# Linear attention beside a gated feed-forward on one core: the weights' side work ordered anew, sums of keys and values stored in whole rows

## The chip, the cores and the metric

One core of one Trainium2 chip runs the whole kernel. The metric is device time in microseconds (us), the median of several executions. Before the change three runs gave 2463.45, 2466.1 and 2470.53 us, so the median is 2466.1 us. The profile is of one further execution.

## The reference, cut to what matters

The input x has 2048 rows of 1024 numbers in fp32. It is normalized, and two branches read it: linear attention with learned feature maps (32 heads of 32), and a SwiGLU feed-forward of width 3584.

```python
xn = (x - mean(x)) / sqrt(var(x) + 1e-5)
q, k, v = xn @ wqkv                              # 32 heads of 32
pq, pk = q @ w_phi, k @ w_phi                    # by head
phi_q = concat(softmax(pq), softmax(-pq))        # 64 features for each head
phi_k = concat(softmax(pk), softmax(-pk))
kv, z = phi_k.T @ v, sum_s(phi_k)                # by head
s = ((phi_q @ kv) / (phi_q @ z + 1e-6)) @ wo
b = (silu(xn @ w1) * (xn @ w3)) @ w2
out = x + s * silu(b)
```

## The kernel before, in words

**Seven products for eight.** A large product is cut into 2x2 blocks and done as seven block products, by the table ORDER: A11 with B11, A12 with B21, S2 with T2, S1 with T1, S3 with T3, S4 with B22 and A22 with T4. S1 to S4 are sums of blocks of x, T1 to T4 sums of blocks of weights. Each fp32 operand is split in two parts: ACT's copy casts to the upper part, DVE's subtraction makes the lower (`split`, L89 to 92). Three passes of the parts make one product, so one step is 12 matmuls of 128x512 (4 blocks of depth by 3 passes).

**First stage: gate and up, 392 steps** (`gate_up`, L573). Two halves of eight row tiles; in each, 28 column blocks f of w1 and w3 by seven products. The accumulators are PSUM banks a, b and c (one, two and two buffers), and what reads a bank (`read`) stands behind its step. Operands from the weights are made four steps ahead by `b_operands` (L262): two sums, then seven splits, with T1 and T4 made on the way.

**The opening** (L670 to 746) is an order written by hand for PE, ACT, DVE, POOL and SP: statistics and norms of eight row tiles, transposes (`first_turn`), splits (`first_split`), sums (`first_sums`) and steps 0 to 3, for which x comes from few tiles. In this stretch POOL makes the weights' sums. Beside it stand folds (`first_folds`, L315): a fold multiplies a block of the weights of keys or queries by the block diagonal of w_phi, so that keys come out of the projection as features' inputs. A fold is a load `wr` or into `room_b`, four matmuls `pw` of 128x128 fp32 (L249; the trace counts eight records), an ACT copy, and a store wk_d or wqo_d. There are 32 folds. Ten of the first 14 stand in the opening, two ahead of each of steps 5 and 6. From step 4 on, steps follow each other.

**Side work by step.** From step 14 the rest runs beside the steps, by a plan that says at which step an instruction is issued (`at`, with `room` which moves a piece to the next step with time left on DVE): four pairs of row tiles of the second half (`side_x`, starting at steps 14, 27, 40 and 53: statistics, transposes, seven splits and their stores xo_d1), the remaining folds (`side_fold`, a load at s0 and the matmuls ahead of step s0+4), eight units of the weights of keys and values (`side_kv`, L473: four loads by `load_kv`, L351, two sums, seven splits with their stores wkv_d), and stores of the first half's operands. Unit m loads at step 64 + 12m.

**What all of these share.** Their blocks come from one pool of 14 buffers (`xp`, tag "x", by `blk`): x's tiles xt and xf, S3, the folds' wr and the units' wkv and t2. Split parts come from another pool, of 11 (`quad`). All DMAs are issued by SP in the order of the program; a load whose buffer is still in use holds SP, and so every DMA behind it.

**Second stage: keys and values** (`heads`, L789): for each half c of the heads, eight pairs of row tiles. `kv` (L779) adds up phi_k.T @ v for 16 heads in one PSUM bank pkv, with two more columns in which a head's sum z lies. When a half is done `kv_out` (L836) copies the sums out: kva on ACT, zs on DVE, then four stores, one after each of the next products. A store is two DMAs of 32 partitions x 4 x 32 into kv_d and two of 32 partitions x 4 x 1 into z_d. For c = 0 they lie inside the second half's products. For c = 1 they lie in the rounds of the third stage.

**Third stage: the product by w2**, rounds r of seven half-size products (L1027, six matmuls each): `a_first` loads hr (512 KB, L881) for the next round and makes the first operands, `a_second` the rest, `load_b` (L874) loads the weights' operands. In rounds 0 to 5 SP's order is the order of the program. Round 1 ends with the last `kv` and `kv_out(1, pkv)`; each of the four rounds behind it issues one store.

**Last stage:** queries, attention by kvu (loaded at L1110) and the output projection. Its `po` products (L1137) read kvu; zb, loaded at L1098, is z spread over the partitions.

Of the kernel before, what the change touches and what calls it, by code (L numbers as in the profile page):

```python
# [17 lines left out]
P = 128  # L18
# [10 lines left out]
def tile_kernel(ctx: ExitStack, tc: tile.TileContext, x, wkT, wqT, wv, wphi, wo, w1, w3, w2, out):  # L29
# [50 lines left out]
    wqo_d = [[dram.tile([P, 2, 512], F, name=f"wqo_d{c}_{k}") for k in range(ND)] for c in range(2)]  # L80
    wo_d = [[dram.tile([P, 2, 512], F, name=f"wo_d{c}_{k}") for k in range(ND)] for c in range(2)]
    w2_d = [{n: dram.tile([P, 2, 2, 512], F, name=f"w2_d{kb}{n}") for n in BNAMES} for kb in range(NKB)]
    kv_d = dram.tile([2, 2, DH, 2 * G, DH], F, name="kv_d")
    z_d = dram.tile([1, 2, 4, 4, 2, DH], F, name="z_d")


# [2 lines left out]
    def split(hi, lo, src, by=None):  # L89

        nc.scalar.copy(hi, src)  # L91
        (by or nc.vector).tensor_sub(lo, src, hi.bitcast(F))  # L92
# [166 lines left out]
        nc.sync.dma_start(rw[:, 1], w3[f].rearrange("p (h k) n -> p h (k n)", h=2))  # L259
        return [rw[:, a, h] for a in range(2) for h in range(2)]  # L260

    def b_operands(rw, bo, eng=None):  # L262
        eng = eng or nc.vector
        b11, b21, b12, b22 = rw
        t2 = work.tile([P, 512], F, name="t2", tag="w")
        b_sums(b11, b12, b22, t2, eng)
        yield
        for _, _, n in ORDER:
            src = {"B11": b11, "B21": b21, "T2": t2, "T1": b11, "T3": b12, "B22": b22, "T4": b21}[n]
            bo[n] = quad("bo")  # L270
            split(bo[n][:, 0], bo[n][:, 1], src.rearrange("p (k n) -> p k n", n=P))
            if n == "B11":
                eng.tensor_sub(b11, b22, t2)
            elif n == "B21":
                eng.tensor_sub(b21, b21, t2)
            yield


# [92 lines left out]
    def at(step, f, d=after):  # L371
        d.setdefault(step, []).append(f)
# [116 lines left out]
    def side_fold(m, s0):  # L489
        wT, k, c, d = folds[m]  # L490
        w = []
        at(s0, lambda: w.append(load_w(wT, k, c)))
        at(s0 + 4, lambda: w.append(flat(fold(w[0], c))), before)
        if m < 16:
            at(s0 + 4, lambda: nc.scalar.copy(flat(w[0]), w[1]))
            at(s0 + 6, lambda: nc.sync.dma_start(d, flat(w[0])))
        else:
            store_quad(s0 + 4, wqo_d[c][k], lambda: w[1], "wqo")

    def side_split(d, src, s0):  # L500
        r = []
# [33 lines left out]
        at(s0, lambda: nc.sync.dma_start(xo_d[0][ANAMES[j]][:, q],  # L535
                                         ao[ANAMES[j]][:, :, :, q * P:(q + 1) * P].bitcast(F)))

    hs, FOLDS = [], 14
    FIRST_STEP = 14
    for i in range(4, 8):  # L540
        side_x(i, FIRST_STEP + 13 * (i - 4))
    for m in range(FOLDS, len(folds)):
        side_fold(m, FIRST_STEP + 40 + 6 * (m - FOLDS))
    for m in range(8):
        side_kv(m // 4, m % 4, FIRST_STEP + 50 + 12 * m)
    for m in range(28):
        side_store(m, FIRST_STEP + 45 + 4 * m)

# [118 lines left out]
        return read  # L667


    for f in range(2):  # L670
        bos[0, f] = {}
        gens[0, f] = b_operands(rws.pop(0), bos[0, f], nc.gpsimd)
    stats(mvs[0], 0, xs[0])
    stats(mvs[0], 1, xs[1])
    r0 = rstd(mvs[0])
# [4 lines left out]
        norm(mvs[0], sd, t, xs[t])  # L680
    stats(mvs[1], 1, xs[3])
    first_turn(0, 0)
    r1 = rstd(mvs[1])
    next(r1)
    first_turn(1, 0)
    first_split("A11", (0,))
    sd = next(r1)
    for t in range(2):
        norm(mvs[1], sd, t, xs[2 + t])
# [10 lines left out]
    for t in (2, 3):  # L700
        first_turn(t, 1)
    reads = [gate_up(0)]
    next(gens[0, 0])
    first_split("A12", (2, 3))
    reads.append(gate_up(1))
    for _ in range(3):
        next(gens[0, 1])
    reads[0]()
    first_folds(1)
    reads.append(gate_up(2))  # L710
    stats(mvs[2], 0, xs[4])
    stats(mvs[2], 1, xs[5])
    r0 = rstd(mvs[2])
    next(r0)
# [4 lines left out]
    for t in range(2):  # L719
        norm(mvs[2], sd, t, xs[4 + t])  # L720
    reads.append(gate_up(3))
    stats(mvs[3], 1, xs[7])
    r1 = rstd(mvs[3])
    next(r1)
# [4 lines left out]
    sd = next(r1)  # L729
    for t in range(2):  # L730
        norm(mvs[3], sd, t, xs[6 + t])
    first_folds(3)
    for t in (6, 7):
        first_turn(t, 0)
        first_turn(t, 1)
    first_sums("S1", (0, 1))
    first_sums("S2", (0, 1))
    first_split("S2", (0, 1))
# [2 lines left out]
    first_split("S2", (2, 3))  # L741
    for f in range(2):
        next(gens[0, f])
    for h in silus:
        nc.scalar.activation(h, h, AF.Silu)
    first_folds(FOLDS - 4 - at_fold)

    def first_late(n):
        ao[n] = slot(0, ANAMES.index(n))
        first_split(n)  # L750

    for k in (5, 6):
        at(k, lambda: first_folds(2), before)
    at(4, lambda: first_split("S1"))
    at(5, lambda: first_sums("S3"))
    at(6, lambda: first_late("S3"))
    at(7, lambda: first_sums("S4"))
# [76 lines left out]
        return pkv, False, last, e1, v1  # L834

    def kv_out(c, pkv):  # L836
        kva = work.tile([P, 8, DH], F, name="kva", tag="h1", bufs=2)
        zs = small.tile([P, 8], F, name="zs")
        nc.scalar.copy(kva, pkv[:, :, :DH])

        nc.vector.tensor_scalar_add(zs[:, :4], pkv[:, :4, DH], 1e-6)
        nc.vector.tensor_copy(zs[:, 4:], pkv[:, 4:, DH])

        def store(j):
            sl = slice(32 * j, 32 * j + 32)
            for s in range(2):
                nc.sync.dma_start(kv_d[j % 2, s, :, G * c + j // 2:G * c + G:2], kva[sl, 4 * s:4 * s + 4])
                nc.sync.dma_start(z_d[0, c, :, j, s].rearrange("g f -> f g"), zs[sl, 4 * s:4 * s + 4])

        return [lambda j=j: store(j) for j in range(4)]  # L850

# [192 lines left out]
    for r, new in enumerate(steps):  # L1046
        kb, i = new or (NKB, 0)
        end = kb == NKB - 1
        if r == 0:
            in_order(ENG.SP)  # L1050
        elif r == 6:
            in_order()
        if new is None:
            in_order(ENG.SP, ENG.Activation, ENG.DVE, ENG.Pool)
            xT = split_q(xf)
        if kb + 1 < NKB and 1 < i < 7:
            load_b(kb + 1, i - 2)
        parts = first
        if r + 1 < len(steps) - 1:
            first = a_first(*steps[r + 1])  # L1060
        bank = {}
        for b, an, bn in TURN:
            if an in FIRST:
                if new:
                    product(kb, i, bank, r, parts[2], b, an, bn)
            elif old:
                product(*old, banks, r, second, b, an, bn)
                if new is None:
                    load_wo(2 * BNAMES.index(bn))
                    load_wo(2 * BNAMES.index(bn) + 1)  # L1070
        if new:
            second = a_second(*parts) if r else ready[1]
        if out_now and r:
            out_now.pop()()
        if r == 1:

            kv(*pend)
            out_now += kv_out(1, pkv)
            late_rw += [rwp.tile([P, 2, 2, 512], R, name="late", tag="rw") for _ in range(2)]
        if i + 1 == len(pairs):  # L1080
            if end:
                for k in range(6):
                    load_wo(k)
            else:
                load_b(kb + 1, 5)
                load_b(kb + 1, 6)


        if end:
            if i:  # L1090
                gate(*pairs[i - 1])
            if i in (1, 2):
                for k in range(4 * i - 4, 4 * i):
                    load_wq(1, k, ring("wq1"))
            if i == 3:
                zb = [flat(ring("zb").bitcast(F)) for _ in range(2)]
                for c in range(2):
                    nc.sync.dma_start(zb[c], z_d[:, c].rearrange("o g j s f -> o (g j s f)").to_broadcast([P, D]))  # L1098
            if 1 < i < 6:
                for j, t in enumerate(pairs[i - 2]):  # L1100
                    load_wq(0, 2 * i - 4 + j, accp.tile([P, 2, 512], R, name="wq0", tag=f"acc{t}"))
            if i == 4:
                xf = load_q(0)
            elif i == 5:
                xT = split_q(xf)
            elif i > 5:
                if i == 6:

                    kvu = work.tile([P, 2 * G, DH], F, name="kvu", tag="h1", bufs=2)
                    nc.sync.dma_start(kvu, kv_d.rearrange("a s f g d -> (a s f) g d"))  # L1110
                es[7 - i] = queries(project_q(xT, 7 - i, "bka"), 7 - i)
            if i == 7:
                xf = load_q(1)
        old, banks = new, bank
# [9 lines left out]
    def attend(c, e):  # L1124


        po = ps.tile([P, 2, 512], F, name="po", tag="po", bufs=1)
        for q in range(2):
            pt = ps.tile([P, 4, P], F, name="pt2", tag="tr", bufs=3)
            for g in range(4):  # L1130
                nc.tensor.transpose(pt[:, g, :], e[:, (4 * q + g) * P:(4 * q + g + 1) * P], ident)  # L1131
            et = work.tile([P, 4, P], F, name="et", tag="w")
            nc.scalar.copy(et, pt)  # L1133
            for g in range(4):
                for hh in range(2):
                    sl = slice(64 * hh, 64 * hh + 64)
                    nc.tensor.matmul(po[32 * g:32 * g + 32, hh, q * P:(q + 1) * P], kvu[sl, G * c + 4 * q + g], et[sl, g],  # L1137
                                     start=True, stop=True, skip_group_check=True)
        oT = quad("oT")
        o4 = oT.rearrange("p u (h q) t -> p u h q t", q=2)  # L1140
        split(o4[:, 0], o4[:, 1], po[:, :, :2 * P].rearrange("p h (q t) -> p h q t", t=P))
        return oT
# [66 lines left out]
```

## Time and profile before

| | |
|---|---|
| median of three runs | 2466.1 us (2463.45 to 2470.53) |
| profiled execution | 2460.08 us, span 2458.3 us |
| granted TensorE clock, mean | 0.994 |
| busy: PE, DVE, ACT, POOL | 2401.5, 1777.1, 881.7, 197.5 us |
| DMA | 518.65 MB, mean 211 GB/s |

PE is the matmul engine, DVE VectorE, ACT ScalarE, POOL GpSimd; SP issues the DMAs. L with a number is a line of the kernel. A row of a timeline has the start, the time, the engine, the line and operation, the output and input, shape, the count, and in brackets the engine's idle time before it with what ended it. SPq is SP's sequencer: its time is that of issuing a DMA. A row of the windows gives, for a stretch, the busy time of PE, PE's weight loads, DVE, ACT and POOL with the count of instructions, then the granted clock, the DMA engines' share and GB/s.

### The profile page before, as it was taken

How to read it: one execution, taken by the hardware profiler on the slowest of the kernel's cores; microseconds unless marked ns; L12 is line 12 of the kernel's file. 1: busy time of each engine (PE TensorE's matmuls, PEld its weight loads, DVE VectorE, ACT ScalarE, POOL GpSimd, SP SyncE). 2: the span in 40 equal slices, each digit the busy share in tenths (PEclk: the TensorE clock that was granted, in tenths of full speed). 3: DMA queues.
4: the chain of work that ended last, by engine and by line, in shares of the span. 5: the costliest groups of instructions: out<-in, count | busy, mean ns of one | idle time of the engine just before them, and what ended most of it. 6: DMA issues, size and time to landing. Idle time of an engine off the chain costs nothing. (4 is left out here: it accounts for less than half of the span.)

```text
span 2458.3 us, 35680 instructions
## 1 busy us (share of the span) xinstructions
PE 2401.5 (98%) x13648; PEld 1969.6 (80%) x13648; DVE 1777.1 (72%) x2893; ACT 881.7 (36%) x1549; POOL 197.5 (8%) x161
## 2 busy tenths in 40 slices
PE   6999989999999999999999998999999999999999
PEld 5888868888888888888787886888888887787777
DVE  7777767876588887764555665578788787777775
ACT  5545434444345454433111123422222243222221
POOL 2000000000000000000000000011111112232222
PEclk9999999999999999999999999999999999999999
DMA  7456879986888886665968756733454376223222
GB/s 269 144 197 233 275 270 319 317 301 220 265 296 305 299 294 230 243 231 213 349 186 330 247 174 154 208 97 135 171 180 172 119 276 233 89 73 96 73 86 69
DMA packets 299514, 518.65 MB, mean 211 GB/s; under 512 B 24400, under 2 KB 171856, under 8 KB 297552
## 3 DMA queue, kind: packets, MB, share of 16 engines
q1 hardware_dynamic: 299344, 516.38, 61.8%
q8 instruction: 107, 1.75, 0.3%
q14 instruction: 63, 0.52, 0.1%
HBM read 330.43 MB, written 185.87 MB: 210 GB/s over the span
## 5 line engine op out<-in xcount | busy, mean ns | idle before, releaser
L92 DVE TENSOR_TENSOR bo<-rw,bo 128x512 fp32r<-128x512 f32 x336 | 232.9, 695 | 163.1 <-ACT bo L91 162.3
L91 ACT CAST bo<-rw 128x512 fp32r<-128x512 f32 x336 | 206.4, 618 | 4.6 <-PE bankb L600 2.2
L1027 PE MATMUL bankb<-bo,as 128*128 128x512 f32 x816 | 201.7, 390 | 1.1 <-DVE acc L1039 1.1
L100 PE MATMUL pm<-wq,xh 128*128 128x512 f32 x768 | 185.5, 394 | 0.0
L1027 PEld LDWEIGHTS bankb<-bo,as 128*128 128x128 f32 x816 | 153.7, 188 | 33.6 <-DVE acc L1039 1.6
L100 PEld LDWEIGHTS pm<-wq,xh 128*128 128x128 f32 x768 | 141.9, 188 | 31.4 <-issue 3.0
L600 PE MATMUL bankb<-op0S,bo 128*128 128x512 f32 x672 | 163.7, 393 | 1.2 <-ACT op0S L91 0.8
L600 PE MATMUL bankb<-op0A,bo 128*128 128x512 f32 x672 | 161.6, 395 | 3.1 <-ACT op0A L91 1.9
L600 PE MATMUL bankc<-op0S,bo 128*128 128x512 f32 x672 | 162.9, 392 | 0.0
L600 PE MATMUL bankb<-op1S,bo 128*128 128x512 f32 x672 | 161.3, 389 | 0.0
L600 PE MATMUL bankc<-op1S,bo 128*128 128x512 f32 x672 | 161.3, 389 | 0.0
L600 PE MATMUL bankb<-op1A,bo 128*128 128x512 f32 x672 | 157.9, 390 | 0.4 <-DVE bo L92 0.2
L1027 PE MATMUL bankc<-bo,as 128*128 128x512 f32 x576 | 147.6, 392 | 8.3 <-ACT acc L1033 8.3
L600 PEld LDWEIGHTS bankb<-op0A,bo 128*128 128x128 f32 x672 | 126.2, 190 | 29.5 <-ACT op0A L91 2.1
L600 PEld LDWEIGHTS bankb<-op0S,bo 128*128 128x128 f32 x672 | 125.7, 189 | 28.1 <-ACT op0S L91 1.2
L600 PEld LDWEIGHTS bankb<-op1A,bo 128*128 128x128 f32 x672 | 125.8, 188 | 27.9 <-DVE u L642 1.2
L600 PEld LDWEIGHTS bankb<-op1S,bo 128*128 128x128 f32 x672 | 126.1, 188 | 26.2
L600 PEld LDWEIGHTS bankc<-op1S,bo 128*128 128x128 f32 x672 | 126.1, 188 | 26.2
L600 PEld LDWEIGHTS bankc<-op0S,bo 128*128 128x128 f32 x672 | 126.1, 189 | 26.2 <-DVE op0S L92 0.3
L100 PE MATMUL pm<-wos,oT 128*128 128x512 f32 x576 | 136.2, 389 | 0.0
L1027 PEld LDWEIGHTS bankc<-bo,as 128*128 128x128 f32 x576 | 108.8, 189 | 31.4 <-ACT acc L1033 8.8
L100 PEld LDWEIGHTS pm<-wos,oT 128*128 128x128 f32 x576 | 108.0, 188 | 22.7 <-issue 0.2
(222 smaller groups left out, 4256.7 us busy)
## 6 DMA issues: line engine op xcount, KB each, us to landing
rw<-in_w SPq DMA_DIRECT2D x112, 512.0 KB, 5.6
hr<-h_d SPq DMA_DIRECT2D x56, 512.0 KB, 3.6
h_d<-h SPq DMA_DIRECT2D x111, 256.0 KB, 5.1
xoS<-xo_d0S SPq DMA_DIRECT2D x32, 512.0 KB, 9.9
xoS<-xo_d1S SPq DMA_DIRECT2D x32, 512.0 KB, 6.6
room<-in_w SPq DMA_DIRECT2D x56, 256.0 KB, 6.9
xoA<-xo_d0A SPq DMA_DIRECT2D x24, 512.0 KB, 8.0
xoA<-xo_d1A SPq DMA_DIRECT2D x24, 512.0 KB, 4.1
```

Of the source, the lines that this page charges most:

```text
L91: nc.scalar.copy(hi, src)
L92: (by or nc.vector).tensor_sub(lo, src, hi.bitcast(F))
L100: nc.tensor.matmul(p, xT[dch][:, a], w(dch, b), start=n == 0, stop=n == 3 * ND - 1)
L600: nc.tensor.matmul(bank[b], bos[tb, f][bn][:, w, k], ao[an][:, u, k], start=first and n == 0, stop=LAST[b] == an and n == 11, skip_group_c ...
L1027: nc.tensor.matmul(bank[b], t[:, u, pos + k], bos[kb, bn, k][:, w], start=first and n == 0, stop=LAST[b] == an and n == 5, skip_group_chec ...
```

## The change

**Sums of keys and values.** kv_d is laid out anew, so that a store of one half is one DMA from kva with 512 bytes for each piece. z is transposed on PE (`pz`, in pkv's bank tag), copied by ACT into zt, and stored by two DMAs of 16 rows of 128 bytes. kv_out returns one store, three DMAs in all, in place of four stores with 16. kvu is loaded by four DMAs, and the index at L1137 follows.

**Side work.** Twelve folds, not 14, stand in the opening. The other 20 load from step 62 on, 5.5 steps apart (before: 18 from step 54, 6 apart), and are used five steps after their load. Unit m of the weights of keys and values loads at step 73 + 11m.

**Opening.** Folds are spread: one behind step 0's matmuls, one ahead of step 2's, two behind step 2's, two behind step 3's, two ahead of and two behind the last transposes, none behind step 4. The two silus of steps 0 and 1 move from ahead of step 4 to step 5. The subtractions that make T1 and T4 (`hold`) wait on POOL until both blocks' sums are done, and POOL's sums of the second block wait, by a copy of one column into `consts`, for the statistics of the fifth row tile. The first row tile's split A11 comes ahead of the second one's transpose.

```diff
-    kv_d = dram.tile([2, 2, DH, 2 * G, DH], F, name="kv_d")
+    kv_d = dram.tile([4, DH, 2, 2, 4, DH], F, name="kv_d")
...
-    def b_operands(rw, bo, eng=None):
+    def b_operands(rw, bo, eng=None, hold=None):
...
+            late = []
             if n == "B11":
-                eng.tensor_sub(b11, b22, t2)
+                late.append(lambda: eng.tensor_sub(b11, b22, t2))
             elif n == "B21":
-                eng.tensor_sub(b21, b21, t2)
+                late.append(lambda: eng.tensor_sub(b21, b21, t2))
+            if hold is not None:
+                hold += late
+            else:
+                for do in late:
+                    do()
             yield
...
-        at(s0 + 4, lambda: w.append(flat(fold(w[0], c))), before)
+        at(s0 + 5, lambda: w.append(flat(fold(w[0], c))), before)
         if m < 16:
-            at(s0 + 4, lambda: nc.scalar.copy(flat(w[0]), w[1]))
-            at(s0 + 6, lambda: nc.sync.dma_start(d, flat(w[0])))
+            at(s0 + 5, lambda: nc.scalar.copy(flat(w[0]), w[1]))
+            at(s0 + 7, lambda: nc.sync.dma_start(d, flat(w[0])))
         else:
-            store_quad(s0 + 4, wqo_d[c][k], lambda: w[1], "wqo")
+            store_quad(s0 + 5, wqo_d[c][k], lambda: w[1], "wqo")
...
-    hs, FOLDS = [], 14
+    hs, FOLDS = [], 12
...
     for m in range(FOLDS, len(folds)):
-        side_fold(m, FIRST_STEP + 40 + 6 * (m - FOLDS))
+        side_fold(m, FIRST_STEP + 48 + 11 * (m - FOLDS) // 2)
     for m in range(8):
-        side_kv(m // 4, m % 4, FIRST_STEP + 50 + 12 * m)
+        side_kv(m // 4, m % 4, FIRST_STEP + 59 + 11 * m)
...
+    held = []
     for f in range(2):
         bos[0, f] = {}
-        gens[0, f] = b_operands(rws.pop(0), bos[0, f], nc.gpsimd)
+        gens[0, f] = b_operands(rws.pop(0), bos[0, f], nc.gpsimd, held)
...
     first_turn(0, 0)
+    first_split("A11", (0,))
+    first_turn(1, 0)
     r1 = rstd(mvs[1])
     next(r1)
-    first_turn(1, 0)
-    first_split("A11", (0,))
...
     reads = [gate_up(0)]
+    first_folds(1)
     next(gens[0, 0])
     first_split("A12", (2, 3))
     reads.append(gate_up(1))
+
+    stats(mvs[2], 0, xs[4])
+    nc.gpsimd.tensor_copy(consts[:, 1:2], mvs[2][:, 0, 0:1])
     for _ in range(3):
         next(gens[0, 1])
+    for do in held:
+        do()
     reads[0]()
     first_folds(1)
     reads.append(gate_up(2))
-    stats(mvs[2], 0, xs[4])
+    first_folds(2)
     stats(mvs[2], 1, xs[5])
...
     reads.append(gate_up(3))
+    first_folds(2)
...
-    first_folds(3)
+    first_folds(2)
     for t in (6, 7):
         first_turn(t, 0)
         first_turn(t, 1)
+    first_folds(2)
...
-    for h in silus:
-        nc.scalar.activation(h, h, AF.Silu)
-    first_folds(FOLDS - 4 - at_fold)
...
-    for k in (5, 6):
-        at(k, lambda: first_folds(2), before)
+    def first_silus():
+        for h in silus:
+            nc.scalar.activation(h, h, AF.Silu)
+
     at(4, lambda: first_split("S1"))
+    at(5, first_silus)
     at(5, lambda: first_sums("S3"))
...
-        kva = work.tile([P, 8, DH], F, name="kva", tag="h1", bufs=2)
+        kvz = work.tile([P, 512], F, name="kvz", tag="h1", bufs=2)
+        kva, zt = kvz[:, :8 * DH], kvz[:8, 8 * DH:8 * DH + P]
         zs = small.tile([P, 8], F, name="zs")
-        nc.scalar.copy(kva, pkv[:, :, :DH])
+        nc.scalar.copy(kva.rearrange("p (m d) -> p m d", d=DH), pkv[:, :, :DH])
...
-        def store(j):
-            sl = slice(32 * j, 32 * j + 32)
+        pz = ps.tile([P, 512], F, name="pz", tag="kv", bufs=1)
+        nc.tensor.transpose(pz[:8, :P], zs, ident)
+        nc.scalar.copy(zt, pz[:8, :P])
+
+        def store():
+            nc.sync.dma_start(kv_d[:, :, :, c].rearrange("j f s m d -> (j f) s (m d)"),
+                              kva.rearrange("p (s n) -> p s n", s=2))
             for s in range(2):
-                nc.sync.dma_start(kv_d[j % 2, s, :, G * c + j // 2:G * c + G:2], kva[sl, 4 * s:4 * s + 4])
-                nc.sync.dma_start(z_d[0, c, :, j, s].rearrange("g f -> f g"), zs[sl, 4 * s:4 * s + 4])
-
-        return [lambda j=j: store(j) for j in range(4)]
+                nc.sync.dma_start(z_d[0, c, :, :, s], zt[4 * s:4 * s + 4].rearrange("g (j f) -> g j f", f=DH))
+
+        return [store]
...
-                    kvu = work.tile([P, 2 * G, DH], F, name="kvu", tag="h1", bufs=2)
-                    nc.sync.dma_start(kvu, kv_d.rearrange("a s f g d -> (a s f) g d"))
+                    kvu = work.tile([P, 2, G, DH], F, name="kvu", tag="h1", bufs=2)
+                    for a in range(2):
+                        for h in range(2):
+                            sl = slice(64 * a + 32 * h, 64 * a + 32 * h + 32)
+                            nc.sync.dma_start(kvu[sl].rearrange("f j g d -> f j (g d)"),
+                                              kv_d[a::2, :, h].rearrange("j f c m d -> f j (c m d)"))
...
-                    nc.tensor.matmul(po[32 * g:32 * g + 32, hh, q * P:(q + 1) * P], kvu[sl, G * c + 4 * q + g], et[sl, g],
+                    nc.tensor.matmul(po[32 * g:32 * g + 32, hh, q * P:(q + 1) * P], kvu[sl, g % 2, 4 * c + 2 * q + g // 2], et[sl, g],
```

On ACT in the opening, from the last transposes of row tiles 2 and 3 to the second square root (sd). xf is a transposed block, bo an operand from weights, op0A one from x, h a copy of a bank; room_b<-pw and wr<-pw are folds. Before:

```order
L222 COPY xf<-pt 128x512 x2
L91 CAST bo<-rw 128x512
L91 CAST op0A_275<-xf 128x4x128 x2
L91 CAST bo<-rw 128x512 x2
L626 COPY h_508<-bankb 128x512
L322 COPY room_b<-pw 128x512
L199 ACTIVATE sd<-mv,consts 128x2
L626 COPY h_551<-bankb 128x512
L199 ACTIVATE sd<-mv,consts 128x2
```

And of the kernel after the change, the same stretch:

```order
L222 COPY xf<-pt 128x512 x2
L328 COPY room_b<-pw 128x512
L91 CAST bo<-rw 128x512
L91 CAST op0A_275<-xf 128x4x128 x2
L91 CAST bo<-rw 128x512 x2
L632 COPY h_521<-bankb 128x512
L328 COPY room_b<-pw 128x512
L328 COPY wr<-pw 128x512 x2
L199 ACTIVATE sd<-mv,consts 128x2
L632 COPY h_576<-bankb 128x512
L328 COPY room_b<-pw 128x512 x2
L199 ACTIVATE sd<-mv,consts 128x2
```

One fold's copy now stands ahead of the casts of step 1's operands, two more ahead of the first square root and two ahead of the second.

On SP in the side work, where a unit of weights loads its four wkv. Of before this is unit 2, at step 88; wr_2905 is the block of the fold ahead of step 94:

```order
L258 DMA rw_2806<-in_w1 128x1024
L259 DMA rw_2806<-in_w3 128x1024
L535 DMA xo_d0A12_89<-op0A12_275 128x8x128
L354 DMA wkv_2857<-wk_d0_2_118 128x512
L355 DMA wkv_2859<-in_wv 128x512
L354 DMA wkv_2858<-wk_d0_6_122 128x512
L355 DMA wkv_2860<-in_wv 128x512
L436 DMA wkv_d0B11_102<-wkvo_2797 256x1x512
L436 DMA wkv_d0B21_103<-wkvo_2826 256x1x512
L242 DMA wr_2905<-in_wqT 128x512
```

After the change unit 1, at step 84, whose loads follow that of a fold's block, wr_2714, which the fold ahead of step 89 reads:

```order
L242 DMA wr_2714<-in_wqT 128x512
L360 DMA wkv_2716<-wk_d0_1_117 128x512
L361 DMA wkv_2718<-in_wv 128x512
L360 DMA wkv_2717<-wk_d0_5_121 128x512
L361 DMA wkv_2719<-in_wv 128x512
L442 DMA xo_d1A11_95<-xoA11_2648 128x1024
L226 DMA xn_d_57<-xf_2679 128x4x128
L502 DMA wk_d1_7_131<-wr_2544 128x512
L442 DMA xo_d1A12_96<-xoA12_2681 128x1024
L226 DMA xn_d_57<-xf_2712 128x4x128
L564 DMA h_d0_2_60<-h0_2514 128x4x128
L564 DMA h_d0_2_60<-h1_2491 128x4x128
```

The unit's loads stood ahead of stores of the unit before and of a fold's load; now they stand ahead of stores of x (xo_d1, xn_d), of a fold (wk_d) and of h.

On SP in the first rounds of the third stage. Before, from round 2's loads, with the first store, to round 3's loads (the four rows kv_d and z_d stand in each of the four rounds 2 to 5):

```order
L874 DMA bo<-w_d1B_187 128x1024 x2
L881 DMA hr<-h_d_0_58 128x1024
L847 DMA kv_d<-kva 32x4x32
L848 DMA z_d<-zs 32x4x1
L847 DMA kv_d<-kva 32x4x32
L848 DMA z_d<-zs 32x4x1
L874 DMA bo<-w_d1B_188 128x1024 x2
L881 DMA hr<-h_d_0_65 128x1024
```

After the change:

```order
L894 DMA bo<-w_d1B_187 128x1024 x2
L901 DMA hr<-h_d_0_58 128x1024
L865 DMA kv_d<-kvz 256x1x128
L868 DMA z_d<-kvz 16x1x32 x2
L894 DMA bo<-w_d1B_188 128x1024 x2
L901 DMA hr<-h_d_0_65 128x1024
L894 DMA bo<-w_d1T_189 128x1024 x2
```

Sixteen DMAs of kv_d and z_d in four rounds have become three in one.

More of the change, by code (lines that the diff above doesn't have):

```diff
@@ L743, in tile_kernel @@
         next(gens[0, f])
-    for h in silus:
-        nc.scalar.activation(h, h, AF.Silu)
-    first_folds(FOLDS - 4 - at_fold)
+    assert at_fold == FOLDS
     def first_late(n):
```

## The prediction, made before the result was known

> **What bounds the kernel now.** I read the windows first. PE is the bound almost everywhere, so only stretches in which it falls behind can give time back (busy PE in the second column, the granted clock third from the end):
>
> ```profile
> span 2458.3 us, 35680 instructions
> 0.00:80.00 80.00, 56.03 (x298) 47.19 (x298) 59.97 (x116) 44.25 (x83) 14.82 (x19) 0.94 0.72 248
> 80.00:300.00 220.00, 220.00 (x1022) 182.63 (x1021) 170.90 (x293) 106.59 (x189) 0.00 (x0) 1.00 0.63 211
> 300.00:400.00 100.00, 89.53 (x408) 74.35 (x407) 71.21 (x112) 44.95 (x83) 0.00 (x0) 0.95 0.87 294
> 400.00:1300.00 900.00, 896.33 (x4700) 739.28 (x4699) 649.44 (x991) 366.70 (x662) 1.83 (x14) 1.00 0.78 268
> 1500.00:1600.00 100.00, 90.51 (x450) 73.89 (x449) 53.80 (x102) 36.66 (x70) 2.59 (x2) 0.95 0.67 165
> ```
>
> Three stretches lose PE time, and the change touches all three: the opening, 24 us of 80; the middle of the first stage, 10.5 of 100; the start of the third stage, 9.5 of 100. Around them PE is full. In each loss the granted clock falls too, so a loss costs its idle time and some slow matmuls behind it.
>
> **The middle.** PE's timeline, then SP's, then one row of ACT and one of the list of transfers (its last column the time from issue to landing):
>
> ```profile
> 304.27 1.05 PE L249 MATMUL pw<-bd,wr 128*128 128x128 f32 x8
> 305.08 2.98 PE L600 MATMUL bankb<-op0S,bo 128*128 128x512 f32 x12
> ...
> 316.06 2.88 PE L600 MATMUL banka<-op0A,bo 128*128 128x512 f32 x12
> 318.78 2.88 PE L600 MATMUL bankb<-op0S,bo 128*128 128x512 f32 x12
> 332.10 2.04 PE L249 MATMUL pw<-bd,wr 128*128 128x128 f32 x8 [10.44 <-DMA wr<-in_wqT]
> 333.80 3.71 PE L600 MATMUL bankc<-op0S,bo 128*128 128x512 f32 x12
> ```
> ```profile
> 302.90 0.42 SPq L535 DMA_DIRECT2D xo_d0A<-op0A  x1
> 316.13 0.33 SPq L354 DMA_DIRECT2D wkv<-wk_d  x1
> ...
> 323.15 0.33 SPq L355 DMA_DIRECT2D wkv<-in_wv  x1
> 323.54 1.26 SPq L436 DMA_DIRECT2D wkv_d0B<-wkvo  x2
> 328.90 0.34 SPq L242 DMA_DIRECT2D wr<-in_wqT  x1
> ```
> ```profile
> 327.53 0.62 ACT L91 CAST wkvo<-wkv 128x512 fp32r<-128x512 f32 x1 [5.16 <-DMA wkv_d0B<-wkvo]
> ```
> ```profile
> wr<-in_wqT SPq DMA_DIRECT2D x3, 256.0 KB, 8.5
> ```
>
> SP issues nothing from 303 to 316 and four loads of unit 2 by 323.15: they wait for blocks of the pool of 14, which the last pair of x still holds. Behind them stand the unit's stores, on which ACT waits (issued from 323.54, landed by 327.53, so 4.0 us from first issue), then the fold's block wr. PE waits for wr 10.44 us. The slow clock adds 2.04 - 1.05 on the fold and 3.71 - 2.88 on the step: 1.8. The stall costs 12.3 us.
>
> **The start of the third stage.** SP's timeline, the transfers, the window, PE's timeline, and rows of the timeline of all engines:
>
> ```profile
> 1512.48 0.38 SPq L881 DMA_DIRECT2D hr<-h_d  x1
> ```
> ```profile
> hr<-h_d SPq DMA_DIRECT2D x4, 512.0 KB, 17.8
> ...
> kv_d<-kva SPq DMA_DIRECT2D x8, 16.0 KB, 9.7
> z_d<-zs SPq DMA_DIRECT2D x8, 0.5 KB, 11.5
> ```
> ```profile
> 1520.00:1530.00 10.00, 4.45 (x20) 3.36 (x18) 0.00 (x0) 0.00 (x0) 0.00 (x0) 0.83 1.02 207
> ```
> ```profile
> 1518.84 1.52 PE L1027 MATMUL bankc<-bo,as 128*128 128x512 f32 x6
> 1532.79 2.93 PE L1027 MATMUL bankc<-bo,as 128*128 128x512 f32 x6 [8.35 <-ACT acc L1033]
> 1535.52 3.53 PE L1027 MATMUL bankb<-bo,as 128*128 128x512 f32 x12
> 1548.36 1.66 PE L1027 MATMUL bankb<-bo,as 128*128 128x512 f32 x6 [1.15 <-DVE acc L1039]
> ```
> ```profile
> 1530.33 0.62 ACT L91 CAST af<-hr 128x512 fp32r<-128x512 f32 x1 [12.05 <-DMA hr<-h_d]
> ```
>
> The named releaser, ACT's copy, had itself waited 12.05 us behind a cast for hr. A store of half a kilobyte takes 11.5 us to land, and hr 17.8 (1512.48 to 1530.3), in a window in which the DMA engines are full at 207 GB/s. PE loses 8.35 + 1.15 idle and, at the slow clock, 2.93 - 1.52 and 3.53 - 2.88 (the twelve matmuls of a step above): 11.6 us.
>
> **The change part by part: stores of the sums.** Thirteen of 16 DMAs go, and kva's pieces of 128 bytes and zs's of 4 become 256 of 512 and 32 of 128. What is added on PE is one transpose of 128x8 for each half. No row shows this shape; between nothing and a quarter of a fold's 1.05 us, I take 0.3 each, the upper end. They wait for zs:
>
> ```profile
> 1509.17 1.20 PE L1027 MATMUL bankb<-bo,af 128*128 128x512 f32 x4
> 1509.77 0.15 DVE L842 COPY zs<-pkv 128x4 f32<-128x4 f32 x1
> ```
>
> The transpose stands behind four matmuls, which end about 1510.3, after zs at 1509.9; zt's copy comes behind an already queued cast on ACT. If that cover were gone, PE would wait about 1 us. For c = 0 PE showed no wait, and nothing is gained. kvu's four loads replace one, with a whole round of products ahead of their first reader; nothing. So the gain is 11.6 - 0.6 = 11.0. Its ends: 0, if the pieces were not the cause, and 12.5, if nothing is added and a last micro-wait goes.
>
> The row says that 16 KB in 128-byte pieces land in 9.7 us and 0.5 KB in 11.5, so cost goes by pieces, not by bytes. The Trainium skill, "DMA: Bandwidth & Descriptors", section "Why small descriptors are slow (HBM only)", gives each packet a small fixed overhead of about three cycles; by that alone, as an estimate, small pieces would be a minor load here, and the sum would be 2460 in place of 2449. That is the second rival.
>
> **The opening.** PE's, ACT's and DVE's timelines:
>
> ```profile
> 24.53 4.15 PE L600 MATMUL bankb<-op0A,bo 128*128 128x512 f32 x10 [1.23 <-DVE op0A L92]
> 28.52 2.91 PE L600 MATMUL banka<-op0A,bo 128*128 128x512 f32 x12
> 55.60 2.07 PE L249 MATMUL pw<-bd,room_b 128*128 128x128 f32 x8 [5.48 <-ACT room_b L322]
> 57.32 3.68 PE L600 MATMUL bankb<-op0S,bo 128*128 128x512 f32 x12
> 73.55 0.73 PE L600 MATMUL bankb<-op0S,bo 128*128 128x512 f32 x2 [0.79 <-ACT op0S L91]
> ```
> ```profile
> 71.32 2.18 ACT L91 CAST op0S<-room_a 128x512 fp32r<-128x512 f32 x4 [2.35 <-DMA wk_d<-room_b]
> ```
> ```profile
> 27.29 3.47 DVE L92 TENSOR_TENSOR bo<-rw,bo 128x512 fp32r<-128x512 f32 x2
> 41.27 1.92 DVE L212 TENSOR_SCALAR late_x<-late_x,mv,sd 128x512 f32<-128x512 f32 x4
> 52.22 1.28 DVE L92 TENSOR_TENSOR bo<-t,bo 128x512 fp32r<-128x512 f32 x2
> ```
>
> I followed the new order by hand with these durations. While POOL makes the weights' sums a DVE subtraction takes 1.74 (27.29's two), later 0.64 (52.22's two); I take POOL for the cause. With POOL held, step 0's matmuls go on at 23.3, 1.2 earlier. Then the third fold's copy on ACT stands ahead of the casts of step 1's operands: step 1 at about 31.0, 2.5 later than 28.52. Folds follow between steps 2 and 3, and their copies ahead of both square roots; the last norms end at 48.6 in place of 43.2 (41.27 + 1.92). From norms to the operands of step 4 it took 10.3 (43.2 to 53.5, the end of the row at 52.22). With about 1 us of waits step 4 starts at 59.9, 2.6 later than 57.32: today it starts late, behind silus and folds on ACT, and that 3.8 of slack takes up the rest. From there steps 4 to 7 stand without the four folds (3.2 us) and without the 2.35 us wait of the split of S3, which stands behind stores from room_b: step 8 at about 72.3, 1.8 earlier than the 73.55 (plus 0.5 of waits, about 74.1). Two of the 14 folds now run beside later steps, where each costs PE 0.81 (304.27 to 305.08): 1.6 back, and 0.2 is left, taken as nothing. Ends: 7 gained, if the copies find ACT free and step 1 isn't late; 5 lost, if two more steps run at half clock.
>
> **Side work.** All units load later, and unit 2's loads come after the last of x's splits; so the stall at 320 as it was goes. But the order shows another of the same kind. At step 84 the fourth load of unit 1 takes the block of wr_2714, which is loaded just ahead of it and read by the fold ahead of step 89. SP stands there until that fold is done. Queued behind are the stores of xo_d1, xn_d and wk_d1_7. At step 88 DVE makes S3 and S1 of the last pair of x in blocks which those stores must leave first. Behind them on DVE is the read of bank b, for which PE's step 90 waits.
>
> From rows: call the fold's end zero. The stores follow from 0.4 us on (0.42 an issue, as at 302.90); wk_d, the fourth, is issued at 1.2 and lands 4.0 later (the wkvo stores above), at 5.2. Three DVE instructions of about 0.65 bring the read to 7.2. PE has step 89 to do, 2.72 us (318.78 less 316.06). So PE is idle 4.5 us and loses about 1.5 at the slow clock, by the 1.8 above: 6.0. What stands further back, the block for the fold ahead of step 94, has four steps of cover left, 10.9 us, against 8.5 to land; nothing, but 5.3 if it is issued only behind DVE's late read, at 7.7 (7.7 + 8.5 - 10.9). The gain is 12.3 - 6.0 = 6.3; the ends are 1 (12.3 - 6.0 - 5.3) and 12.3 (DVE does not come late).
>
> **The sum.** 2460.1 - 0 - 6.3 - 11.0 = 2442.8 for an execution like the profiled one, which took 2460.08 (span 2458.3 and 1.8 around it). The median of the three runs is 6.0 above it, at 2466.1. So 2442.8 + 6.0 = 2448.8, forecast 2449.
>
> **The rivals.**
> 1. The middle's stall stays as large: SP's hold at step 84 delays the fold's block of step 94 as well, PE waits twice, and 5.3 of the 6.3 go: 2454. For it: SP's backlog stands ahead of that block, stores of h among it, which wait for DVE.
> 2. Small pieces are not the cause: hr was late since bo, hr and the late loads together filled the engines (207 GB/s at full share). Then the 11.0 go: 2460. Against it: hr brings 512 KB, which at 207 GB/s is 2.5 us, and three such loads issued together, 1.5 MB, would be done in 7.6, not in 17.8. The rule of the Trainium skill named above, of a small fixed overhead, would make this rival of it.
> 3. The opening loses about 6: ACT's fold copies ahead of casts and square roots are later than reckoned, and the steps after run at half clock as the 4.15 at 24.53 does: 2455.
> 4. The opening gains about 7: 2442.
> 5. Slower: the hold of SP repeats at every later unit. Each unit's last load could again take a block that a fold still has to read; if the six units from the third on lose as the one at step 84 does, 6 x 6 = 36 is added: 2485. It turns the sign from 17.3 / 6 = 2.9 us a unit on. Against it: later waits name blocks of steps well past, and from 400 to 1300 PE lost only 3.7 of 900 us.
>
> **How the numbers follow.** A measurement of this kernel can tell about 0.3% from no change, 7.4 us. The forecast has 0.52, with a range of its own of 2442 to 2455 (middle 1 to 12.3 and opening within 3). Rival 1 has 0.12, rival 2 0.08, rival 3 0.10, rival 4 0.12 and rival 5 0.06. Faster by over 0.3% (below 2458.7) are all but 2 and 5; of those a small part of 1 and 3 falls within 0.3%, and part of rival 2 to faster: 0.85 faster, 0.09 the same, 0.06 slower. The range reaches from 2438, where the middle costs nothing (6 less) and 5 of rival 4's 7 come too, to 2459, with rivals 1 and 3 and the edge of rival 2 inside; rival 5, most of 2 and the tails are left out, under 2 in 10.
>
> **What the profile after would show.** Right: the start of the third stage has hr landing in under 8 us and no wait of PE over 2; SP's row for the fourth wkv load of unit 1 stands behind a fold at step 89, and PE waits 3 to 6 us at step 90 with ACT or DVE as the releaser; the opening's step 4 starts at 58 to 62 and step 8 at 70 to 75. Wrong: hr still late beside three DMAs (rival 2), a wait for wr as long as before (1), or waits that repeat every 11 steps from 100 on (5).

## The result

The kernel after takes 2447.38 us, the median of six runs (2445.02 to 2449.6); before takes 2466.23 in six (2463.45 to 2470.53). The ratio is 0.9923, with an interval of 0.991 to 0.9936: faster, by 16 to 22 us. The forecast was 2449. One of the ten executions of before_new_opening below took 5340.17 us, far outside the other nine (2465.17 to 2469.96), and is left out of its ratio.

### The profile after

The profiled execution took 2447.39 us. First the windows, with the columns as before:

```profile
span 2445.6 us, 35679 instructions
0.00:80.00 80.00, 54.20 (x278) 44.91 (x279) 55.87 (x115) 42.44 (x80) 14.53 (x20) 0.89 0.70 235
80.00:300.00 220.00, 220.00 (x1017) 182.40 (x1017) 170.06 (x291) 106.99 (x190) 0.00 (x0) 1.00 0.59 199
300.00:400.00 100.00, 93.76 (x430) 77.55 (x428) 75.11 (x118) 46.82 (x86) 0.00 (x0) 0.98 0.92 315
1500.00:1600.00 100.00, 100.00 (x503) 82.49 (x503) 62.72 (x115) 41.66 (x80) 5.18 (x4) 1.00 0.47 170
```

The start of the third stage is full now (90.51 before), the middle has a smaller hole (93.76 in place of 89.53), and the opening has 1.8 us less of busy PE (54.20 in place of 56.03, at a clock of 0.89), of which 1.6 are the two folds that moved out of it.

**The third stage.** PE's timeline, then the list of transfers between 1508 and 1550:

```profile
1508.77 1.19 PE L1047 MATMUL bankb<-bo,af 128*128 128x512 f32 x4
1509.80 0.27 PE L861 MATMUL pz<-ident,zs 128*8 128x128 f32 x1
1509.82 0.70 PE L1047 MATMUL bankb<-bo,af 128*128 128x512 f32 x2
```
```profile
hr<-h_d SPq DMA_DIRECT2D x5, 512.0 KB, 5.3
kv_d<-kvz SPq DMA_DIRECT2D x1, 128.0 KB, 2.1
```

hr lands in 5.3 us, where it took 17.8, the transpose costs 0.27, and PE waits for nothing. To compare runs I take one number from PE's timeline: the time from the start of the last pkv group to the start of the 301st product matmul of this stage behind it (without the transpose). It is 80.82 us before and 68.97 after: 11.85 less.

**The middle.** SP's timeline, then DVE's, then PE's:

```profile
293.44 0.32 SPq L360 DMA_DIRECT2D wkv<-wk_d  x1
307.97 0.33 SPq L361 DMA_DIRECT2D wkv<-in_wv  x1
308.39 0.38 SPq L442 DMA_DIRECT2D xo_d1A<-xoA  x1
308.87 0.39 SPq L226 DMA_DIRECT2D xn_d<-xf  x1
309.35 1.14 SPq L502 DMA_DIRECT2D wk_d<-wr  x1
```
```profile
313.83 0.69 DVE L232 TENSOR_TENSOR s<-xf 128x512 f32<-128x512 f32 x1 [6.64 <-DMA wk_d<-wr]
314.55 0.69 DVE L234 TENSOR_TENSOR xf<-xf 128x512 f32<-128x512 f32 x1
315.16 0.68 DVE L648 TENSOR_TENSOR u<-bankb,u 128x512 f32<-128x512 f32 x1
```
```profile
306.89 1.05 PE L249 MATMUL pw<-bd,wr 128*128 128x128 f32 x8
307.69 2.98 PE L606 MATMUL bankc<-op0S,bo 128*128 128x512 f32 x12
315.90 7.19 PE L606 MATMUL bankb<-op0A,bo 128*128 128x512 f32 x24 [5.23 <-DVE u L648]
```

The rows read as a chain. SP issues nothing between 293.8 and 307.97, where the fold ends; wk_d goes out fourth, at 309.35; DVE's sum S3 waits for it until 313.83 and the read of bank b until 315.16; PE waits 5.23. Two steps, 24 matmuls, take 5.60 at full clock, here 7.19, so the stall costs 6.8, where the old one cost 12.3.

**The opening.** PE's timeline, one row of ACT's, one of DVE's, then the row of PE with which step 12 begins in the profile of before:

```profile
23.09 2.56 PE L606 MATMUL bankb<-op0A,bo 128*128 128x512 f32 x10 [0.25 <-DVE op0A L92]
...
52.60 1.86 PE L249 MATMUL pw<-bd,wr 128*128 128x128 f32 x8 [2.29 <-DMA wr<-in_wkT]
60.56 8.70 PE L606 MATMUL bankb<-op0S,bo 128*128 128x512 f32 x24 [6.10 <-ACT bo L91]
69.10 5.60 PE L606 MATMUL bankc<-op0S,bo 128*128 128x512 f32 x24
74.54 0.61 PE L606 MATMUL bankb<-op0S,bo 128*128 128x512 f32 x2
...
86.10 8.32 PE L606 MATMUL bankb<-op0A,bo 128*128 128x512 f32 x36
```
```profile
54.50 0.59 ACT L328 COPY wr<-pw 128x512 f32<-128x512 f32 x1 [3.57 <-PE pw L249]
```
```profile
45.56 1.92 DVE L212 TENSOR_SCALAR late_x<-late_x,mv,sd 128x512 f32<-128x512 f32 x4
```
```profile
85.30 8.32 PE L600 MATMUL bankb<-op0A,bo 128*128 128x512 f32 x36
```

Step 4 starts at 60.56 and steps 4 and 5 run at the slow clock, 8.70 in place of 5.60. Step 8 starts at 74.54 and step 12 at 86.10, 0.8 later than before (85.30). One profile says little here: in the eight profiles with this opening (after, after_old_stores, before_new_opening, small_kv, small_z, both z_extra kernels and unit_a_step_later, all below) step 12 starts between 82.97 and 87.70, on average at 85.3, and in the three with the old one at 85.30, 85.37 and 85.60. So up to step 12 the new opening gains and loses nothing on average.

**Where the two profiles differ.** Their spans differ by 12.7 us: 12.3 behind the last pkv group and 0.4 ahead of it. Ahead of it the middle gives 5.5 and the opening takes 0.8 and two folds 1.6; the other 2.7 are lost behind the middle and at the start of the second stage, mostly in small waits. The medians differ by 18.9. The rest lies with the execution of before that was profiled (2460.08, below its six timed runs), as the experiments show.

### The profile page after: what moved, and what is told of

Same layout as the page of the kernel before. It is cut to its first block, busy times and chain, and to the rows that moved or that the text cites. A ratio compares the mean times of both kernels' runs of the same rounds, so it can differ in the third digit from the quotient of the medians.

```text
span 2445.6 us, 35679 instructions
## 1 busy us (share of the span) xinstructions
PE 2401.9 (98%) x13650; PEld 1969.5 (81%) x13650; DVE 1774.3 (73%) x2893; ACT 882.6 (36%) x1551; POOL 197.1 (8%) x162
```

## The experiments

Each is timed in rounds with the kernel before on the same chip; in the table the ratio is to that, with its interval. Before itself took 2465.83 us beside the four kernels from after_old_stores to before_new_opening, 2463.56 beside small_kv, small_z, unit_a_step_later and folds_behind_splits, and 2463.8 beside the other four, so medians of different groups can differ by some 2.7 us for no reason of the kernel's; small_kv and z_extra_spread, which turn out as after did, stand in for it in their groups.

| kernel | us | ratio to before |
|---|---|---|
| after | 2447.38 | 0.9923 (0.991 to 0.9936) |
| after_old_stores | 2462.82 | 0.9986 (0.9976 to 0.9996) |
| before_new_stores | 2452.57 | 0.9948 (0.9934 to 0.9963) |
| before_new_side | 2460.68 | 0.9987 (0.9977 to 0.9996) |
| before_new_opening | 2467.63 | 1.0004 (0.9994 to 1.0014) |
| small_kv | 2447.53 | 0.9928 (0.9913 to 0.9942) |
| small_z | 2460.0 | 0.9985 (0.9975 to 0.9995) |
| z_extra_dense | 2461.11 | 0.9983 (0.9973 to 0.9992) |
| z_extra_spread | 2447.54 | 0.9926 (0.9908 to 0.9944) |
| unit_a_step_later | 2440.68 | 0.9903 (0.9888 to 0.9917) |
| folds_behind_splits | 2444.4 | 0.9915 (0.99 to 0.993) |
| hold_undone | 2452.06 | 0.9943 (0.9922 to 0.9965) |
| both_mended | 2434.81 | 0.9876 (0.9858 to 0.9894) |

### The three parts of the change, each by itself

after_old_stores and before_new_stores exchange `kv_out`, kv_d's layout, kvu's load and the index at L1137. before_new_side takes the two lines of the plan and the folds' steps, before_new_opening everything in the opening, with FOLDS = 12. The two lines of the plan:

```diff
-        side_fold(m, FIRST_STEP + 40 + 6 * (m - FOLDS))
+        side_fold(m, FIRST_STEP + 48 + 11 * (m - 12) // 2)
...
-        side_kv(m // 4, m % 4, FIRST_STEP + 50 + 12 * m)
+        side_kv(m // 4, m % 4, FIRST_STEP + 59 + 11 * m)
```

> The kernel after, with the 16 small stores of before put back (kv_d's layout, kv_out and kvu's load of before). If the small pieces are the cause of the wait at the start of the third stage, its 11.6 us come back in the profile: PE waits about 8 us for hr there, hr lands in about 18 us, and the time is about 2459 (2447.4 + 11.6). The six microseconds by which the timed runs of before lie above its profiled one may belong to the same wait: then about 2465. Rival, that the pieces are not the cause: 2447 to 2449.

> The kernel before, with only the new stores of the sums (one of whole rows, two of z transposed). If the pieces are the cause: the start of the third stage has no wait of PE over 1 us, and the time is 2466 - 12 = 2454; 2448 if the six microseconds between profile and timed runs of before lie in this wait too. Rival, that the pieces are not the cause: 2466.

> The kernel before, with only the new plan of the side work (folds half a dozen steps later and 5.5 steps apart, units of the weights of keys and values from step 73 on, 11 apart); the opening keeps its 14 folds, and the stores are the old ones. By the two profiles the stall ahead of step 94 (10.4 us idle) goes and one ahead of step 90 of about 5 us idle comes: 12.3 - 6.8 = 5.5 less, 2461. If the six microseconds between profile and timed runs lie in the old stall: 2455. Rival, that the stall moves and does not shrink: 2466.

> The kernel before, with only the new opening (12 folds spread among the first steps, the held subtractions on POOL, the silus at step 5); the two folds that it gives up load at steps 42 and 48. By the two profiles step 12 starts 0.8 us later, and two folds more beside the steps cost 1.6: 2466 + 2.4 = 2468.6. The stall ahead of step 94 stays as before. Rival, that the opening as a whole gains what the forecast's other case had (7): 2459.

By the ratios times 2466 the stores give 12.8 us, the side plan 3.2 and the opening takes 1.0 (not told from nothing: its interval is -1.5 to +3.5). The sum, 15.0, and the whole, 19.0 (15.8 to 22.2), agree within their intervals. Put back into the kernel after, the old stores take 15.5. PE's timeline of after_old_stores and of before_new_opening shows how the old loss varies:

```profile
1532.53 2.93 PE L1043 MATMUL bankc<-bo,as 128*128 128x512 f32 x6 [9.61 <-ACT acc L1049]
...
1561.04 2.92 PE L1043 MATMUL bankb<-bo,as 128*128 128x512 f32 x6 [3.35 <-DVE acc L1055]
```
```profile
1540.42 2.93 PE L1043 MATMUL bankc<-bo,as 128*128 128x512 f32 x6 [10.26 <-ACT acc L1049]
```

The measure above (68.97 us with the new stores, in both kernels that have them) is 80.82 (before), 82.22 (before_new_side), 83.19 (before_new_opening) and 88.24 (after_old_stores) with the old ones: a loss of 11.9 to 19.3, and the profile of before had the smallest. The times with the old stores also lie further apart: 2458.35 to 2467.47 in ten executions of after_old_stores, 2450.97 to 2454.27 in four of before_new_stores.

before_new_side's PE timeline has the stall of after, in the same place; before_new_opening's has the old one:

```profile
313.36 8.47 PE L600 MATMUL bankb<-op0A,bo 128*128 128x512 f32 x24 [5.21 <-DVE u L642]
```
```profile
336.17 2.04 PE L249 MATMUL pw<-bd,wr 128*128 128x128 f32 x8 [10.32 <-DMA wr<-in_wqT]
```

In before_new_side the 24 matmuls behind the wait take 8.47, so there the stall costs 8.1 and the plan gives 4.2 in the profile. So each stall belongs to its plan of the side work, and neither the stores nor the opening moves it.

### Which pieces cost

small_kv stores kva in its old pieces of 128 bytes and z in rows; small_z stores kva in rows and z in its old pieces of 4 bytes. Its store, with two DMAs of z in each of four rounds:

```diff
+        def store(j):
+            sl = slice(32 * j, 32 * j + 32)
+            if j == 3:
+                nc.sync.dma_start(kv_d[:, :, :, c].rearrange("j f s m d -> (j f) s (m d)"), ...)
+            for s in range(2):
+                nc.sync.dma_start(z_d[0, c, :, j, s].rearrange("g f -> f g"), zs[sl, 4 * s:4 * s + 4])
```

> The kernel after, with kva stored in pieces of 128 bytes again (8 DMAs in four rounds, 1024 pieces for each half) and z still in whole rows. If the loss goes by the number of pieces: half of it comes back, about 6 to 7 us, 2454. If the 4-byte pieces of z carry it: PE waits under 2 us at the start of the third stage and the time is 2447 to 2449. If the bytes carried it, these would (128 KB against 4 KB): 2459 or more.

> The kernel after, with z stored in pieces of 4 bytes again (8 DMAs in four rounds, 1024 pieces for each half, no transpose) and kva still in one store of whole rows. If the loss goes by the number of pieces: about 6 to 7 us come back, 2454. If the 4-byte pieces carry it: about 12 or more, 2460. If the bytes: 2447 to 2449.

The list of transfers between 1508 and 1550, of small_kv and of small_z:

```profile
hr<-h_d SPq DMA_DIRECT2D x5, 512.0 KB, 3.4
kv_d<-kvz SPq DMA_DIRECT2D x8, 16.0 KB, 5.7
```
```profile
hr<-h_d SPq DMA_DIRECT2D x4, 512.0 KB, 17.6
z_d<-zs SPq DMA_DIRECT2D x7, 0.5 KB, 11.4
```

1024 pieces of 128 bytes cost nothing that can be measured (2447.53), 1024 pieces of 4 bytes cost all of it (2460.0, the same ratio as with all the old stores), with about as many DMAs (8 and 2 for each half in the one, 1 and 8 in the other). So neither the count of pieces nor the bytes decides. The next pair asks whether it is their size or where they lie. Both kernels keep the new stores and add eight for each half, of 4-byte pieces into a tensor zj that nothing reads; the two differ in one number:

```diff
+    zj = dram.tile([2, 4, 4, 2, DH, 1], F, name="zj")
...
+                nc.sync.dma_start(zj[c, :, j, s, :, 0:1].rearrange("g f o -> f g o"), zs[sl, 4 * s:4 * s + 4].unsqueeze(2))
```

The last dimension of zj is 1 in z_extra_dense and 128 in z_extra_spread, so that a piece's neighbour lies 4 or 512 bytes away.

> The kernel after with its own stores, and beside them eight more for each half as the old stores of z were: pieces of 4 bytes, side by side in a tensor that nothing reads, two in each of four rounds. Nothing that is needed goes through them. If such stores alone make the loss: about 12.6 more than after, 2460, as with z stored so. If the loss came of something else in that run, such as the missing transpose: 2447 to 2448.

> The same eight extra stores of 4-byte pieces, but each piece 512 bytes from the next in the tensor that nothing reads. If pieces of 4 bytes cost by their size alone, whatever lies beside them: 2460 as with the dense ones. If they cost because many of them fall into the same small stretch of memory: near 2448, as 128-byte pieces do.

The same list, of the dense kernel and of the spread one, each with the line of SP's queue (packets, MB, and their time as a share of that of the 16 engines):

```profile
q1 hardware_dynamic: 3093, 6.10, 83.2%
...
hr<-h_d SPq DMA_DIRECT2D x4, 512.0 KB, 12.9
...
zj<-zs SPq DMA_DIRECT2D x8, 0.5 KB, 16.0
```
```profile
q1 hardware_dynamic: 3336, 6.96, 47.1%
...
hr<-h_d SPq DMA_DIRECT2D x5, 512.0 KB, 4.7
...
zj<-zs SPq DMA_DIRECT2D x8, 0.5 KB, 5.4
```

Side by side such a store lands in 16.0 us and holds up hr; 512 bytes apart it lands in 5.4 and the kernel takes 2447.54, as if the stores weren't there. The pieces do not differ in number: under 512 bytes 1381 packets go over in this stretch in the one and 1416 in the other. Yet the dense ones hold the engines for 83.2% of it, while fewer bytes move, and the spread ones for 47.1%. The measure above is 81.07 with the dense ones, 12.1 more, and 68.97 with the spread ones. The loss comes of many tiny pieces in one small stretch of memory. Why they hinder one another there, and from what distance they don't, these runs don't show.

### The stall in the middle

```diff
-        side_kv(m // 4, m % 4, FIRST_STEP + 59 + 11 * m)
+        side_kv(m // 4, m % 4, FIRST_STEP + 59 + 11 * m + (m == 1))
```

> The kernel after, with the loads of the second unit of the weights of keys and values one step later, at 85 in place of 84; nothing else changes. By the theory (its fourth load takes the block of the fold ahead of step 89 and holds SP until then) that load now finds another block: SP issues its loads and the stores behind them at once, the wait of 5.2 us ahead of step 90 goes with its slow matmuls, 6.8 us in all, and the time is about 2441. Rival, that DVE is late at step 90 because of its own work or the transfers: the wait stays within 1 us and the time is 2446 to 2448. In the order DVE's sum S3 at step 88 now waits for that fold itself, which may leave up to 1 us of wait.

2440.68, 6.7 less than after and 6.9 less than small_kv beside it (4.9 by the ratios), by one step for one load of one unit. SP's, DVE's and PE's timelines:

```profile
291.92 0.41 SPq L360 DMA_DIRECT2D wkv<-wk_d  x1
294.86 0.33 SPq L361 DMA_DIRECT2D wkv<-in_wv  x1
```
```profile
306.43 0.69 DVE L232 TENSOR_TENSOR s<-xf 128x512 f32<-128x512 f32 x1 [0.79 <-PE pw L249]
```
```profile
308.96 5.60 PE L606 MATMUL bankb<-op0A,bo 128*128 128x512 f32 x24
```

The fourth load waits 2.5 us, not 14. S3 now waits for the fold itself, 0.79, and PE's steps 90 and 91 take 5.60 with no wait.

### The opening

folds_behind_splits moves one call; hold_undone gives `b_operands` no list, so that POOL subtracts at once, as before:

```diff
-    first_folds(2)
     first_sums("S1", (0, 1))
...
     for f in range(2):
         next(gens[0, f])
+    first_folds(2)
```
```diff
-        gens[0, f] = b_operands(rws.pop(0), bos[0, f], nc.gpsimd, held)
+        gens[0, f] = b_operands(rws.pop(0), bos[0, f], nc.gpsimd)
```

> The kernel after, with the opening's last two folds moved from ahead of the sums S1 and S2 to behind the splits of S2. By the profile the split S2 stands on ACT behind the last fold's copy, which waits 3.6 us for a fold whose block lands late. Without that, step 4 starts 3 to 4 us earlier (57 in place of 60.6), step 8 2 to 3 us earlier, and the time is 2444 to 2445. Rival, that steps 4 to 7 only move and the wait comes back at the split of S3 or S4, which the folds' copies now stand ahead of: step 12 starts within 0.5 us of 86.1 and the time is 2447.

> The kernel after, with POOL's subtractions for T1 and T4 made as early as before (in the profile of before POOL ran them beside the first splits). If POOL slows DVE there, as the prediction took it: DVE's subtractions in the first splits take 1.2 to 1.7 us again in place of 0.64, step 0's matmuls go on about 1.2 us later than 23.1, step 1 up to 1 us later, and the time is 2448 to 2449. If the later steps' slack takes it up: 2447 within 0.7.

PE's timeline of folds_behind_splits, then PE's, DVE's and POOL's of hold_undone, and the row of DVE in after:

```profile
53.41 1.81 PE L249 MATMUL pw<-bd,wr 128*128 128x128 f32 x8 [2.16 <-DMA wr<-in_wkT]
56.49 7.83 PE L606 MATMUL bankb<-op0S,bo 128*128 128x512 f32 x24 [1.26 <-ACT bo L91]
...
81.27 8.32 PE L606 MATMUL bankb<-op0A,bo 128*128 128x512 f32 x36
```
```profile
24.26 4.64 PE L606 MATMUL bankb<-op0A,bo 128*128 128x512 f32 x10 [1.22 <-DVE op0A L92]
...
34.51 4.63 PE L606 MATMUL banka<-op0A,bo 128*128 128x512 f32 x10 [1.24 <-DVE op0A L92]
...
91.30 8.32 PE L606 MATMUL bankb<-op0A,bo 128*128 128x512 f32 x36
```
```profile
32.09 2.37 DVE L92 TENSOR_TENSOR op0A<-xf,op0A 128x512 fp32r<-128x512 f32 x2
```
```profile
32.25 1.66 POOL L276 TENSOR_TENSOR rw<-rw,t 128x512 f32<-128x512 f32 x1 [10.40 <-DVE bo L92]
```
```profile
28.33 1.29 DVE L92 TENSOR_TENSOR op0A<-xf,op0A 128x512 fp32r<-128x512 f32 x2
```

With the folds behind the splits the late block (2.16) no longer holds ACT's split of S2: step 4 starts at 56.49, and step 12 at 81.27, ahead of all eight profiles above. The time is 2444.4, 3.0 less, but the intervals of the two ratios overlap (0.99 to 0.993 and 0.991 to 0.9936), so the gain in time isn't clear of noise; in its profile, whose span is only 1.0 shorter than after's, part of it is lost again at the turn of the halves, in a wait of 2.57 in place of 0.74. The hold on POOL is worth more than expected: without it the time is 2452.06, 4.7 more than after and 4.5 more than z_extra_spread beside it. Two DVE subtractions beside POOL's take 2.37 in place of 1.29, now at step 1 too, whose matmuls wait 1.24 and run at half speed (4.63 for ten); step 12 starts at 91.30, 5.2 later than in after's profile and 3.6 later than in the latest of the eight.

> The kernel after, with both amendments: the second unit's loads one step later and the opening's last two folds behind the splits of S2. Apart they gave 6.7 and 3.0 us. If they add up: 2437.7. If the second is partly eaten by the wait at the turn of the halves, which in its profile was 2.6 us and in that of after 0.7: 2438 to 2440.

both_mended has both edits and takes 2434.81, below the 2437.7 of a plain sum and below both kernels. In its profile step 12 starts at 82.22, 3.9 earlier than in after's, and the wait at the turn of the halves is gone; why it comes out 2.9 below the sum isn't shown, but the opening alone varies by 4.7 from profile to profile. Its window from 300 to 400:

```profile
300.00:400.00 100.00, 99.00 (x461) 82.33 (x460) 79.83 (x125) 48.21 (x88) 0.00 (x0) 1.00 0.94 327
```

## Why the prediction was right

**The stores: right in place and size, wrong in what costs.** The term was -11.0; the two profiles give -11.85, the timed exchanges -12.8 and -15.5. The step "cost goes by pieces, not by bytes" failed: 1024 pieces of 128 bytes cost nothing measurable, and 1024 of 4 bytes cost all or nothing by where they lie. Of the rule in the Trainium skill, "DMA: Bandwidth & Descriptors", section "Why small descriptors are slow (HBM only)", a small fixed overhead for each packet, the spread pieces and those of 128 bytes fit it (2447.54 and 2447.53); the dense ones don't (2461.11). The same page's "Specifications" has transfers under 512 bytes done by read-modify-write. Size alone is not what costs here, since the spread pieces of 4 bytes are under it too.

**The middle: right as a mechanism, 0.8 us off.** The gain was put at 6.3 and is 5.5 in the profiles (timed alone, the plan gives 3.2, with 1.0 to 5.7 as its interval), since the new stall is 6.8 and not 6.0: wk_d was issued 1.4 us behind the fold's end (307.94) in place of 1.2 and landed 4.5 later in place of 4.0; idle 5.23 for 4.5, slow clock 1.6 for 1.5. The fold ahead of step 94 had its block in time, and no later unit brought a stall back, so rivals 1 and 5 did not come.

**The opening: the start of step 4 right by luck, the rest not.** Step 4 came at 60.56, forecast 59.9. But the last norms ended at 47.48 (45.56 + 1.92), forecast 48.6, and from there it took 13.1, forecast 11.3, as the late fold held ACT; the two errors nearly cancel. "Step 8 at about 72.3, 1.8 earlier" failed: it is 74.54. The working had steps 4 and 5 at full clock (5.60, measured 8.70), and no wait of the last fold for its block (2.29), which ACT's split of S2 stood behind. So 0 was forecast and some 2.4 are lost in the profile (0.8 and 1.6), or the 1.6 of the two folds alone by the average of the eight; timed, the loss isn't clear of noise. POOL's hold was put at 1.2 and is worth about 4.7.

**The step from profile to median: luck.** For an execution like the profiled one the sum gave 2442.8, and after's took 2447.39, 4.6 more: the middle gave 0.8 less than forecast, the opening took 2.4 and the small waits 2.7, while the part behind the last pkv group gave 1.3 more. The 6.0 added on top was taken as the same for both kernels. It is not: after's profiled run is its median (2447.39 and 2447.38). So an error of 4.6 and one of 6.0 nearly cancel, which makes 2449 look better than its terms were. At least part of the 6.0 belongs to the removed loss, which is larger in the profiles of the other kernels with the old stores (up to 19.3) than in that of before (11.9).

## What to carry to other kernels

When many small results go to memory, do not store them as pieces of a few bytes side by side: write whole rows, by a transpose if need be. One that costs 0.27 us on the matmul engine removed some 12; pieces of 128 bytes needed no mending here. In a plan where many users share a pool of buffers and one queue issues all loads, ask of each load which buffer it will get: one step's shift of one load was worth 6.7 us. Give an engine's copy no place behind a transfer that may be late when the main chain runs through that engine.

## What the runs showed of the hardware that was not expected

- Stores of 128 pieces of 4 bytes landed in 16.0 us with neighbours 4 bytes apart and in 5.4 with 512, beside the same loads; the dense ones delayed a load of 512 KB from 4.7 us to 12.9.
- Beside POOL's subtractions two of DVE took 2.37 us in place of 1.29. The Trainium skill, "GPSIMD Engine Reference", section "1. Specifications", says that the two engines share their way to SBUF, for DVE's instructions with two inputs from it; the runs agree.
